# Inverse over k2: another PSUM bank, two copies, and sums between SBUF operands

## The chip, the cores and the metric

The kernel runs on one core of a Trainium2 chip. The metric is device time in microseconds (us) of one execution; the median of three runs before the change was 2562.01 us (2561.42 to 2562.07). The trace shown here comes from one profiled execution.

## What is computed

The input x has 8 batches of 3008 positions and 256 features. A spectral layer comes first: a real Fourier transform over the positions, a complex product with a 256 x 256 matrix plus bias, soft thresholding, and the inverse transform. Its output goes row by row through a gated feed-forward network (FFN).

```python
X = np.fft.rfft(x, axis=1)
Yr = Xr @ w_r - Xi @ w_i + b_r
Yi = Xr @ w_i + Xi @ w_r + b_i
Y = np.sign(Y) * np.maximum(np.abs(Y) - 0.01, 0.0)   # Yr and Yi apart
y = np.fft.irfft(Yr + 1j * Yi, n=3008, axis=1)
out = (silu(y @ w_gate) * (y @ w_val)) @ w_out       # 256 -> 1536 -> 256
```

## The kernel before, in words

The program has two stages. The transform (`transform`, until about 520 us) computes the spectral layer, with 3008 split as 47 x 64 so that each Fourier transform is a pair of small matrix products. The FFN (`gated_ffn`) follows and is not touched by the change.

The transform works in units that overlap like a pipeline. For each batch, 8 chunks of input are multiplied by a Fourier matrix over 47 (`first`, L516, PSUM banks ps_a and ps_z) and transposed by VectorE (`turn`, L521). For each of 96 pairs of k1 follow the transform over 64 (`second`, L558), the split of its result into a high and a low part (L606 to L611), three products with the weights (`sum`, L565, in PSUM bank ps_s; `mix`, L580), the addition of the bias (`spread`, L569, which reads ps_s), the copy to SBUF (`gather` and `rest`, L591), and the thresholding (`clip` L617, `shrink` L618).

The inverse over k2 (`backs`, L619 to L662) takes one pair or two pairs in turn, 64 times. `back` (L639) multiplies the real half into one PSUM bank and the imaginary half into a second; for the first 53 these are ps_x0 and ps_x1, for the last 11 ps_a and ps_z. Then `keep` (L643, ScalarE) copies the imaginary half to SBUF, and `plus` and `minus` (L648, VectorE) form sum and difference of the real half in PSUM and the copy. `store` (L653) sends the result z to DRAM.

The inverse over k1 (`unit`, 56 times in the transform) loads z back, multiplies (`tiles`, L711) into the same banks ps_x0 and ps_x1, and copies both out (`xt0`, `xt1`, L723, on ScalarE or VectorE, each 376 columns). So `back` has to wait for the copies of the `tiles` before it (`own`, L626), and `tiles` for the `minus` of the last `back` (`free`, L756). On TensorE the three stand in the fixed order `tiles`, `first`, `back` (`then`, `soon`).

All of this is written as named steps with needs, an estimated cost, one or more engines and a key. A list scheduler (`Plan.order`) gives each engine its order: a step starts when its needs are met, and of those that could start the one with the least key goes first. `SHIFT` (by kind), `LATER` (by kind and range) and `NUDGE` (by name) move keys, in slots of 5.5 us; `BIAS` moves the choice between engines. A step may take and free a named resource (`takes`, `frees`), and `wide` marks VectorE steps for which the planner reckons with GpSimd. Each engine runs its steps in the order found. In the head (`head`, L367) the loads of batch 0's chunks, of wa, wj and wr, and of bias and wf have keys too; the order found before is wa, wj, wr, then the eight chunks.

Of the kernel before, what the change touches and what calls it, by code (L numbers as in the profile page):

```python
# [9 lines left out]
F32 = mybir.dt.float32  # L10
# [3 lines left out]
ALU = mybir.AluOpType  # L14
# [31 lines left out]
SHIFT = {'add': -0.5, 'lower': -2.68, 'third': -0.5, 'turn5': -0.45, 'turn4': -0.36, 'turn0': 0.85, 'y_hi': -0.37, 'f': -1.7, 'out': 5.65, 'spread': -0.67, 'back': 2.36, 'raw': -0.72, 'second': -6.01, 'y_lo': 0.68, 'shrink': -1.75, 'z_in': 3.81, 'mix': 0.52, 'wr': -16.97, 'turn1': 0.1, 'tiles': 0.76, 'turn6': -0.16, 'wo': 9.39, 'x_sum': 4.59, 'sum': -2.3, 'flat_lo': -1.55, 'xt1': -4.21, 'x': 2.74, 'store': 0.3, 'turn': 1.34, 'wm': -32.33, 'bits down': -0.5, 'upper': 3.57, 'wj': -17.49, 'kept': -6.94, 'negate': -11.43, 'turn3': -2.97, 'unit': 10.52, 'wm_hi': -10.71, 'z': 0.5, 'bias': 6.32, 'wi_lo': -0.06, 'turn2': -1.38, 'x_hi': 2.79, 'clip': -0.54, 'xt0': 0.88, 'wa': -15.83, 'warm': 7.15, 'bits up': -1.5, 'f_lo': -0.43, 'wm_lo': 4.79, 'wi': -0.1, 'f_hi': 2.5, 'wf': -0.48, 'rest': 2.68, 'first': -1.1, 'bits': -0.71, 'flat_hi': 4.03, 'sums': -0.64, 'x_first': -4.78, 'early': 7.49, 'keep': 2.85, 'xf': -0.91, 'x_lo': 10.96, 'minus': -0.48, 'gather': 4.93, 'f_sum': -4.37, 'plus': 0.33}  # L46
# [3 lines left out]
    ('f_lo', 66, 80, 1.25),  # L50
    ('turn', 4, 16, 0.37),
    ('clip', 26, 38, 0.62),
    ('xt0', 26, 47, -0.76),
    ('second', 42, 72, -0.49),
    ('rest', 73, 76, 0.14),
    ('first', 8, 16, 0.25),
    ('turn3', 5, 10, -1.0),
    ('bits', 7, 14, -1.12),
    ('turn0', 8, 14, -1.0),
    ('x', 15, 19, -1.0),  # L60
    ('turn', 12, 14, -0.25),
    ('tiles', 67, 68, -0.5),
    ('out', 12, 15, 0.25),
    ('kept', 8, 11, -0.12),
    ('turn4', 11, 12, -0.5),
    ('turn3', 3, 5, 0.12),
    ('back', 7, 10, 0.12),
# [260 lines left out]
def transform(ctx, tc, front, ring, last, ps_, feed, xp, w_r, w_i, cb, wup_raw, wdn_raw, ca, cf, ci, cq, w21, wup_d, wdn_d, xt_d, d2):  # L328
# [201 lines left out]
    def pair(b, p):  # L530

        made = {}

        def tile(name, shape, dtype, tag, **kw):
            if name not in made:
                made[name] = sb.tile(shape, dtype, name=tag, tag=tag, **kw)
            return made[name]

        first = lambda x: x[:, :2].rearrange("p q c (k b) -> p (c k) q b", b=64)
        blocks = lambda x: x.rearrange("p (a b) -> p a b", b=64)  # L540
        flat = lambda x: x[:, 2].rearrange("p c a -> p (c a)")
        both = lambda: made["ps_b"].rearrange("p (a q b) -> p a q b", q=2, b=64)
        total = lambda: tile("f", [P, 2 * P], F32, "f", bufs=2)
        f_hi = lambda: tile("f_hi", [P, 3, 2, P], F32R, "f_hi", bufs=3)
        f_lo = lambda: tile("f_lo", [P, 3, 2, P], F32R, "f_lo", bufs=3)
        t = lambda: made_t.__setitem__(j, tile("t", [P, T], F32, "t", bufs=4)) or made_t[j]
        y = lambda: tile("y", [P, T], F32, "y", bufs=2)
        mixb = mixed[p % 2]

        def second(part=slice(0, 2)):  # L550
            if part.start == 0:
                made["ps_b"] = ps_.tile([P, T], F32, name="ps_b", tag="ps_b")
            ps = made["ps_b"]
            src = d1[b % 2][:, p]
            for cc in range(2)[part]:
                for k in range(2):
                    s = (cc * 2 + k) * P
                    nc.tensor.matmul(ps[:, s : s + P], lhsT=src[:, cc * P : (cc + 1) * P, k], rhs=wf[:, 2 * p + k, :], start=True, stop=True)  # L558

        def total_product():  # L560
            p1 = made["ps_s"] = ps_.tile([P, T], F32, name="ps_s")
            n = 0
            for cc in range(2):
                for w, x in PASSES:
                    nc.tensor.matmul(p1[:, :C], lhsT=(f_hi, f_lo)[x]()[:, 2, cc, :], rhs=wmix[0][w][:, cc, :], start=n == 0, stop=n == 5)  # L565
                    n += 1

        def spread():
            v.tensor_tensor(  # L569
                mixb.rearrange("p (a c) -> p a c", c=C),  # L570
                made["ps_s"][:, :C].rearrange("p (a c) -> p a c", a=1).to_broadcast([P, 2, C]),
                bias[0],
                op=ALU.add,
            )

        def mix():
            for half, (q, i) in enumerate(((1, 2), (0, 1))):
# [36 lines left out]
        add("mix", "PE", 1.45, 2.4, [now("spread"), now("f_lo")], mix)
        add("gather", "ACT", 0.74, 2.7, [now("mix"), back_of(j - 4) if j >= 4 else None], lambda: gather(0), tail=0.0)
        add("rest", "ACT", 0.74, 2.72, [now("gather")], lambda: gather(1), tail=0.0)
        add("clip", "DVE", 0.34, 2.95, [now("rest"), old("shrink", 2)], lambda: v.tensor_scalar(y(), t(), LAM, -LAM, op0=ALU.min, op1=ALU.max), wide=True)  # L617
        add("shrink", {"DVE": 0.61} if j > B * NP - 3 else {"POOL": 1.23, "DVE": 0.61}, None, 3.0, [now("clip")], lambda eng=v: eng.tensor_tensor(t(), t(), y(), op=ALU.subtract), wide=True)  # L618
    def backs(i):  # L619

        js = [3 * i // 2] if i % 2 == 0 else [3 * i // 2, 3 * i // 2 + 1]
        k = i + BEHIND
        n = len(js)
        box = {}
        key = 1.5 * k * SLOT
# [577 lines left out]
```

## Time and profile before

| what | value |
|---|---|
| median of 3 runs | 2562.01 us |
| profiled execution | 2560.62 us |
| span of its trace | 2558.5 us |
| mean granted TensorE clock | 0.999 |
| busy: TensorE / VectorE / GpSimd / ScalarE | 99% / 80% / 79% / 64% |

The span is the time from the first to the last instruction; the profiled execution is 2.1 us longer and 1.4 us shorter than the median. TensorE's matrix products overlap, and the ends that the profile gives are modelled, so its busy share hides short waits; the distance from one step's start to the next one's start shows them. PE is TensorE, PEld its weight loads, DVE VectorE, ACT ScalarE, POOL GpSimd, SP the engine that issues DMAs.

### The profile page before, as it was taken

To read this page: it belongs to the slowest core of one execution; us is meant where nothing else is said; L and a number is where in the kernel's file an instruction comes from. 1 tells how busy PE (TensorE), PEld (TensorE's weight loads), DVE (VectorE), ACT (ScalarE), POOL (GpSimd) and SP (SyncE) were. 2 spreads that over 40 slices of the span, in tenths; PEclk is the share of its full clock that TensorE was granted. 3 is DMA by queue.
4 is the path that set the end of the run, shared out by engine and by line. 5 is a ranking of instruction groups with operands and counts; after the bars stand their busy time and mean duration, and the time that the engine had idled before them with its cause. 6 is when DMAs were issued, how large, how long until landed. Compare 5 with 4: busy or idle time off the path is not lost.

```text
span 2558.5 us, 46813 instructions
## 1 busy us (share of the span) xinstructions
PE 2533.3 (99%) x16990; PEld 2101.3 (82%) x16990; DVE 2056.0 (80%) x3075; ACT 1626.3 (64%) x3188; POOL 2029.6 (79%) x1572
## 2 busy tenths in 40 slices
PE   8999999999999999999999999999999999999999
PEld 6777778878888888888888888888888888888899
DVE  6998888668777877887888788878787888788787
ACT  4676766756666666666666666665666566666665
POOL 4776665568888888888888888888888888888886
PEclk9999999999999999999999999999999999999999
DMA  6889887855445445544544444444444444444453
GB/s 212 270 272 284 288 283 249 269 204 192 164 156 170 158 158 160 168 154 148 167 163 150 142 163 163 150 142 163 163 149 142 158 163 146 142 160 159 150 183 123
DMA packets 134886, 460.55 MB, mean 180 GB/s; under 512 B 13824, under 2 KB 59904, under 8 KB 134656
## 3 DMA queue, kind: packets, MB, share of 16 engines
q1 hardware_dynamic: 134512, 457.46, 53.8%
q8 instruction: 135, 2.21, 0.3%
q14 instruction: 95, 0.78, 0.1%
q10 hardware_dynamic: 144, 0.10, 0.0%
HBM read 366.54 MB, written 90.96 MB: 179 GB/s over the span
## 4 chain that ended last, share of the span: by engine, by line
PE 79%; DVE 0%; ACT 0%; issue 0%; DVEq 0%; ACTq 0%
PE bank L860 79%; PE bank L1104 0%; PE ps_x L711 0%; DVE bank L1033 0%; DVE z L648 0%; PE ps_t L639 0%; DVE o L941 0%; DVE bank L1055 0%; DVE hidden L1055 0%; ACT part L643 0%; ACT xt L723 0%; DVEq L1193 0%; DVEq L1033 0%; ACTq L643 0%
## 5 line engine op out<-in xcount | busy, mean ns | idle before, releaser
L860 PE MATMUL bank<-x_near,wup 128*128 128x512 f32 (+1 forms) x4032 | 1035.7, 386 | 1.6 <-DVE z L648 1.0
L880 POOL TENSOR_TENSOR h_parts<-more,h_parts 128x512 fp32r<-128x512 f32 (+1 forms) x572 | 846.9, 1494 | 101.2 <-ACT h_parts L876 100.5
L860 PEld LDWEIGHTS bank<-x_near,wup 128*128 128x128 f32 x4032 | 750.9, 188 | 154.1 <-DVE bank L1033 4.1
L860 PE MATMUL bank<-h_parts,wdn 128*128 128x512 f32 (+1 forms) x3024 | 835.1, 385 | 0.0
L880 POOL TENSOR_TENSOR h_parts<-hidden,h_parts 128x512 fp32r<-128x512 f32 (+1 forms) x431 | 563.4, 1316 | 220.2 <-ACT h_parts L876 199.5
L860 PEld LDWEIGHTS bank<-h_parts,wdn 128*128 128x128 f32 x3024 | 564.8, 188 | 108.5 <-POOL h_parts L880 0.3
L876 ACT CAST h_parts<-hidden 128x512 fp32r<-128x512 f32 (+1 forms) x433 | 265.4, 613 | 451.7 <-DVE hidden L1006 451.7
L860 PE MATMUL bank<-x_parts,wup 128*128 128x512 f32 (+1 forms) x2016 | 525.5, 384 | 0.0
L1006 DVE TENSOR_TENSOR hidden<-hidden,bank 128x512 f32<-128x512 f32 (+1 forms) x576 | 376.1, 674 | 77.8 <-PE bank L860 69.5
L860 PEld LDWEIGHTS bank<-x_parts,wup 128*128 128x128 f32 x2016 | 375.4, 188 | 71.6 <-DVE bank L1033 1.7
L901 DVE TENSOR_TENSOR sums<-sums,bank 128x512 f32<-128x512 f32 (+1 forms) x357 | 240.3, 673 | 234.3 <-PE bank L860 234.3
L876 ACT CAST h_parts<-more 128x512 fp32r<-128x512 f32 (+1 forms) x572 | 349.3, 611 | 38.2 <-DVE more L871 27.0
L1004 ACT ACTIVATE hidden<-bank 128x512 f32<-128x512 f32 (+1 forms) x432 | 252.1, 584 | 115.4 <-PE bank L860 114.1
L871 DVE TENSOR_TENSOR more<-hidden 128x512 f32<-128x512 f32 (+1 forms) x286 | 291.2, 1057 | 0.0
L871 DVE TENSOR_TENSOR more<-hidden,more 128x512 f32<-128x512 f32 (+1 forms) x286 | 257.3, 900 | 0.0
L1011 ACT COPY bank<-bank 128x512 f32<-128x512 f32 (+1 forms) x288 | 161.6, 561 | 110.0 <-DVE hidden L1006 104.1
L1033 DVE TENSOR_TENSOR bank<-hidden,bank 128x512 f32<-128x512 f32 (+1 forms) x288 | 197.0, 684 | 39.4 <-PE bank L860 27.0
L618 POOL TENSOR_TENSOR t<-t,y 128x512 f32<-128x512 f32 x94 | 126.4, 1345 | 99.5 <-DVE y L617 87.9
L1019 ACT COPY hidden<-bank 128x512 f32<-128x512 f32 (+1 forms) x288 | 167.6, 582 | 2.4
L591 ACT COPY t<-mixb 64x256 f32<-64x256 f32 x384 | 140.7, 366 | 33.6 <-PE mixb L580 27.6
L284 POOL TENSOR_TENSOR x_near<-xf,x_near 128x512 fp32r<-128x512 f32 (+1 forms) x112 | 141.1, 1275 | 5.0 <-PE bank L860 4.8
L1055 DVE TENSOR_TENSOR hidden<-hidden,bank 128x512 f32<-128x512 f32 (+1 forms) x144 | 97.4, 676 | 43.9 <-PE bank L860 43.7
(94 smaller groups left out, 2868.3 us busy)
## 6 DMA issues: line engine op xcount, KB each, us to landing
wup<-wup_d SPq DMA_DIRECT2D x288, 896.0 KB, 4.6
scratch<-xp SPq DMA_DIRECT2D x59, 512.0 KB, 5.7
out<-o SPq DMA_DIRECT2D x88, 256.0 KB, 6.1
d<-z SPq DMA_DIRECT2D x84, 256.0 KB, 4.1
xt_d<-xt SPq DMA_DIRECT2D x56, 376.0 KB, 6.3
z_in<-d SPq DMA_DIRECT2D x98, 192.0 KB, 4.7
xf<-xt_d SPq DMA_DIRECT2D x15, 1024.0 KB, 6.8
wup_d<-wup SPq DMA_DIRECT2D x12, 896.0 KB, 5.0
```

The source lines that it names most:

```text
L284: low = lambda: eng.tensor_tensor(part[:, 1, :h], src, f32(part[:, 0, :h]), op=ALU.subtract)
L591: nc.scalar.copy(t()[64 * half : 64 * half + 64, k * C : (k + 1) * C], mixb[64 * k : 64 * k + 64, half * C : (half + 1) * C])
L860: nc.tensor.matmul(o, lhsT=weights[w], rhs=parts[x], start=start and i == 0, stop=stop and i == 2, skip_group_check=True)
L871: v.tensor_tensor(at(o, h), at(a, h), at(b, h), op=ALU.subtract)
L876: act.copy(pair[i][:, 0, :h], at(i, h))
L880: eng.tensor_tensor(pair[i][:, 1, :h], at(i, h), f32(pair[i][:, 0, :h]), op=ALU.subtract)
L901: v.tensor_tensor(o, o, spare[:, :h], op=ALU.add)
L1004: act.activation(at(i, h), src, AF.Silu)
L1006: v.tensor_tensor(at(i, h), at(i, h), src, op=ALU.mult)
L1011: act.copy(b3[:, :h], b1[:, :h])
L1019: act.copy(m5, b2[:, :h])
L1033: v.tensor_tensor(b2[:, :h], m5, b3[:, :h], op=ALU.add)
```

## The change

The imaginary half of the first 53 inverses over k2 goes to ps_s, the bank of `sum`, in place of ps_x1. `back` therefore needs `xt0` alone of the copies before it, and it shares the named resource "sums" with `sum`: `sum` takes it and `spread` frees it, `back` takes it and `keep` frees it. Both halves are now copied out of PSUM (`hold` for the real half, into z itself; `keep` for the imaginary half), each on ScalarE or VectorE. `minus` comes before `plus`, both read SBUF alone, and each may run on GpSimd or VectorE; `store` waits for `plus`. They are not marked `wide`. The next `back` waits for both copies, and the next `tiles` for `hold` and for the two xt copies before it.

All tables of keys are other ones. `NUDGE` has 24 entries (1620 before), `LATER` 21 (18 before), and `SHIFT` has other values for nearly every kind; the entries for the head's loads and weights ('wr', 'wj', 'wm', 'wm_hi', 'wa') go from between -10.7 and -32.3 slots to between -1.0 and 0.06, and 'x_first', 'early', 'wi', 'wf' and 'wm_lo' have none. With these keys the chunks of batch 0 stand ahead of wr and wj, and chunk 0 ahead of wa.

```diff
-        add("sum", "PE", 0.73, 1.3, [now("flat_lo"), old("spread", 1)], total_product)
-        add("spread", "DVE", 0.61, 1.45, [now("sum"), old("rest", 2)], spread)
+        add("sum", "PE", 0.73, 1.3, [now("flat_lo"), old("spread", 1)], total_product, takes="sums")
+        add("spread", "DVE", 0.61, 1.45, [now("sum"), old("rest", 2)], spread, frees="sums")
...
-        own = [f"xt0 {k - APART}", f"xt1 {k - APART}"] if APART <= k < PAIRS else []
+        own = [f"xt0 {k - APART}"] if APART <= k < PAIRS else []
...
-        before = [f"minus {i - 1}"] if i else []
+        before = [f"hold {i - 1}", f"keep {i - 1}"] if i else []
...
-            box["ps"] = [... for tag in (("ps_x0", "ps_x1") if k < PAIRS else ("ps_a", "ps_z"))]
+            box["ps"] = [... for tag in (("ps_x0", "ps_s") if k < PAIRS else ("ps_a", "ps_z"))]
...
-        def keep():
+        def copy(to, src, eng):
+            (nc.scalar.copy if eng is None else eng.tensor_copy)(to, src[:, : n * C])
+
+        def hold(eng):
+            box["z"] = sb.tile([P, 2, T], F32, name="z", tag="z", bufs=2)
+            copy(box["z"][:, 0, : n * C], box["ps"][0], eng)
+
+        def keep(eng):
             box["part"] = sb.tile([P, T], F32, name="part", tag="part", bufs=2)
-            nc.scalar.copy(box["part"][:, : n * C], box["ps"][1][:, : n * C])
-
-        def join(s, op):
-            if not s:
-                box["z"] = sb.tile([P, 2, T], F32, name="z", tag="z", bufs=2)
-            v.tensor_tensor(box["z"][:, s, : n * C], box["ps"][0][:, : n * C], box["part"][:, : n * C], op=op)
+            copy(box["part"][:, : n * C], box["ps"][1], eng)
+
+        def join(s, op, eng):
+            eng.tensor_tensor(box["z"][:, s, : n * C], box["z"][:, 0, : n * C], box["part"][:, : n * C], op=op)
...
-        plan.add(f"keep {i}", "ACT", 0.28 if n == 1 else 0.48, key + 0.4 * SLOT, ...)
-        plan.add(f"plus {i}", "DVE", 0.34 if n == 1 else 0.61, key + 0.5 * SLOT, [f"keep {i}"] + old, lambda: join(0, ALU.add))
-        plan.add(f"minus {i}", "DVE", 0.34 if n == 1 else 0.61, key + 0.55 * SLOT, [f"plus {i}"], lambda: join(1, ALU.subtract))
+        out_of = {"ACT": 0.28, "DVE": 0.34} if n == 1 else {"ACT": 0.48, "DVE": 0.61}
+        both = {"POOL": 0.7, "DVE": 0.34} if n == 1 else {"POOL": 1.23, "DVE": 0.61}
+        plan.add(f"hold {i}", out_of, None, key + 0.4 * SLOT, [f"back {i}"] + old, hold)
+        plan.add(f"keep {i}", out_of, None, key + 0.42 * SLOT, [f"back {i}"] + ([f"plus {i - 2}"] if i > 1 else []), keep, frees="sums" if k < PAIRS else None)
+        plan.add(f"minus {i}", both, None, key + 0.5 * SLOT, [f"keep {i}", f"hold {i}"], lambda eng: join(1, ALU.subtract, eng))
+        plan.add(f"plus {i}", both, None, key + 0.55 * SLOT, [f"minus {i}"], lambda eng: join(0, ALU.add, eng))
...
-        free = [f"minus {i - 1}"] if i > 0 and k <= PAIRS else []
+        free = ([f"hold {i - 1}"] if i > 0 and k <= PAIRS else []) + ([f"xt0 {k - 1 - APART}", f"xt1 {k - 1 - APART}"] if k > APART else [])
```

The biases of the new steps are 'hold DVE': 0.5, 'keep DVE': 1.1, 'minus DVE': -0.2, 'plus DVE': -1.5 (us added to the time at which VectorE would end, for the choice alone); that of 'xt0 DVE' is 3.8 and that of 'xt1 DVE' 1.1, where there were none. In `SHIFT`, 'hold' has 4.09 slots and 'keep' -0.58.

## Rows read from the trace of the kernel before

**Rows 1.** The page: span of the program, and the chain that ended last.

```profile
span 2558.5 us, 46813 instructions
...
PE bank L860 79%; PE bank L1104 0%; PE ps_x L711 0%; DVE bank L1033 0%; DVE z L648 0%; PE ps_t L639 0%; DVE o L941 0%; DVE bank L1055 0%; DVE hidden L1055 0%; ACT part L643 0%; ACT xt L723 0%; DVEq L1193 0%; DVEq L1033 0%; ACTq L643 0%
```

**Rows 2.** Windows: busy us of PE, PEld, DVE, ACT, POOL (instructions); clock; DMA share; GB/s.

```profile
0.00:24.00 24.00, 19.16 (x113) 8.05 (x114) 10.67 (x18) 4.77 (x8) 6.89 (x10) 0.86 0.79 289
...
95.00:450.00 355.00, 345.17 (x5441) 280.37 (x5441) 308.78 (x579) 244.96 (x596) 235.29 (x232) 1.00 0.87 278
```

**Rows 3.** Waits of PE's weight loads, 95 to 450 us: total, times, longest.

```profile
PEld ps_t L639 <- ACT xt L723: 22.2, 20, 1.3
PEld ps_t L639 <- DVE xt L723: 16.1, 22, 1.3
```

**Rows 4.** Timeline, three inverses: start, length, engine, line, operation [idle before].

```profile
311.51 1.07 PE L516 MATMUL ps_a<-scratch,wa 48*64 48x512 f32 x8
...
311.80 0.85 ACT L723 COPY xt<-ps_x 128x376 f32<-128x376 f32 x2
...
312.70 1.09 PE L639 MATMUL ps_t<-t,wi 64*64 64x256 f32 x16
...
339.75 1.07 PE L516 MATMUL ps_a<-scratch,wa 48*64 48x512 f32 x8
...
340.64 1.04 PE L639 MATMUL ps_t<-t,wi 64*64 64x256 f32 x16
...
349.19 1.07 PE L516 MATMUL ps_a<-scratch,wa 48*64 48x512 f32 x8
...
350.68 0.66 PE L639 MATMUL ps_t<-t,wi 64*64 64x256 f32 x8 [0.42 <-ACT xt L723]
```

**Rows 5.** Groups by line, 95 to 450 us: busy, mean | idle before.

```profile
L618 POOL TENSOR_TENSOR t<-t,y 128x512 f32<-128x512 f32 x68 | 92.5, 1361 | 67.0 <-DVE y L617 60.3 <-PE ps_a L516 6.7
...
L648 DVE TENSOR_TENSOR z<-ps_t,part 128x256 f32<-128x256 f32 (+1 forms) x90 | 47.8, 536 | 2.5 <-ACT part L643 2.1
...
L723 ACT COPY xt<-ps_x 128x376 f32<-128x376 f32 x66 | 29.2, 478 | 9.4 <-PE ps_x L711 7.8 <-ACT t L591 0.9
...
L643 ACT COPY part<-ps_t 128x512 f32<-128x512 f32 (+1 forms) x44 | 21.1, 479 | 22.3 <-PE ps_t L639 21.9
```

**Rows 6.** One line, 600 to 2500 us: VectorE operation with both operands in SBUF.

```profile
L871 DVE TENSOR_TENSOR more<-hidden x268: 544/949/1782, 604.2 to 2496.4; 128x512 f32<-128x512 f32 x127, 128x384 f32<-128x384 f32 x7
```

**Rows 7.** Timeline around the inverse at 312.70 us.

```profile
312.77 0.69 DVE L569 TENSOR_TENSOR mixb<-ps_s,bias 128x512 f32<-128x512 f32 x1
...
313.89 0.58 ACT L643 COPY part<-ps_t 128x512 f32<-128x512 f32 x1 [0.94 <-PE ps_t L639]
...
314.69 0.36 PE L565 MATMUL ps_s<-wm_hi,f_hi 128*128 128x256 f32 x1
```

**Rows 8.** Timeline of the head.

```profile
1.19 0.42 SPq L402 DMA_DIRECT2D wj<-w_i  x1
...
2.17 0.47 SPq L384 DMA_DIRECT2D scratch<-xp  x1
...
8.42 1.09 PE L516 MATMUL ps_a<-scratch,wa 48*64 48x512 f32 x8 [1.88 <-DMA scratch<-xp]
...
16.85 5.04 DVE L521 STREAM_TRANSPOSE d<-ps_a 128x512 f32<-128x512 f32 x8 [0.53 <-PE ps_a L516]
...
21.95 0.74 PE L558 MATMUL ps_b<-wf,d 128*128 128x128 f32 x4 [0.17 <-DVE d L521]
```

**Rows 9.** Timeline of the step from transform to FFN.

```profile
517.57 1.38 PE L711 MATMUL ps_x<-wo,z_in 48*64 48x47 f32 x64
...
517.92 0.58 ACT L643 COPY part<-ps_t 128x512 f32<-128x512 f32 x1 [0.17 <-PE ps_t L639]
518.54 1.29 DVE L648 TENSOR_TENSOR z<-ps_t,part 128x512 f32<-128x512 f32 x2 [2.00 <-ACT part L643]
...
519.97 1.63 PE L860 MATMUL bank<-x_near,wup 128*128 128x512 f32 x6 [1.03 <-DVE z L648]
```

More of the change, by code (lines that the diff above doesn't have):

```diff
@@ L45 @@
 FEED = 84
-SHIFT = {'add': -0.5, 'lower': -2.68, 'third': -0.5, 'turn5': -0.45, 'turn4': -0.36, 'turn0': 0.85, 'y_hi': -0.37, 'f': -1.7, 'out': 5.65, 'spread': -0.67, 'back': 2.36, 'raw': -0.72, 'second': -6.01, 'y_lo': 0.68, 'shrink': -1.75, 'z_in': 3.81, 'mix': 0.52, 'wr': -16.97, 'turn1': 0.1, 'tiles': 0.76, 'turn6': -0.16, 'wo': 9.39, 'x_sum': 4.59, 'sum': -2.3, 'flat_lo': -1.55, 'xt1': -4.21, 'x': 2.74, 'store': 0.3, 'turn': 1.34, 'wm': -32.33, 'bits down': -0.5, 'upper': 3.57, 'wj': -17.49, 'kept': -6.94, 'negate': -11.43, 'turn3': -2.97, 'unit': 10.52, 'wm_hi': -10.71, 'z': 0.5, 'bias': 6.32, 'wi_lo': -0.06, 'turn2': -1.38, 'x_hi': 2.79, 'clip': -0.54, 'xt0': 0.88, 'wa': -15.83, 'warm': 7.15, 'bits up': -1.5, 'f_lo': -0.43, 'wm_lo': 4.79, 'wi': -0.1, 'f_hi': 2.5, 'wf': -0.48, 'rest': 2.68, 'first': -1.1, 'bits': -0.71, 'flat_hi': 4.03, 'sums': -0.64, 'x_first': -4.78, 'early': 7.49, 'keep': 2.85, 'xf': -0.91, 'x_lo': 10.96, 'minus': -0.48, 'gather': 4.93, 'f_sum': -4.37, 'plus': 0.33}
+SHIFT = {'add': -0.5, 'lower': 3.45, 'third': -0.5, 'turn5': -2.56, 'turn4': -0.52, 'turn0': -0.23, 'y_hi': -0.37, 'f': 1.24, 'out': -2.32, 'spread': -1.87, 'back': 1.18, 'raw': -5.24, 'second': -4.82, 'y_lo': 0.68, 'shrink': -5.54, 'z_in': 0.06, 'mix': 0.55, 'wr': -1.0, 'turn1': 0.2, 'tiles': 0.94, 'turn6': -0.34, 'wo': 0.06, 'x_sum': 7.6, 'sum': -4.95, 'flat_lo': 1.38, 'xt1': 1.43, 'x': 3.03, 'store': -0.91, 'turn': 3.45, 'wm': -0.12, 'bits down': -0.5, 'upper': 2.97, 'wj': -0.12, 'kept': -7.82, 'negate': 0.25, 'turn3': 1.92, 'unit': -14.47, 'wm_hi': -0.12, 'z': 0.5, 'bias': -0.44, 'wi_lo': -0.06, 'turn2': 0.71, 'x_hi': 4.92, 'clip': 0.55, 'xt0': 0.98, 'wa': 0.06, 'warm': 0.25, 'bits up': -1.5, 'f_lo': 0.92, 'f_hi': 1.87, 'rest': 4.15, 'first': 4.34, 'bits': 1.7, 'flat_hi': 3.89, 'sums': 2.92, 'keep': -0.58, 'xf': 6.58, 'x_lo': -4.03, 'minus': 2.83, 'gather': 5.4, 'f_sum': -2.09, 'plus': 0.04, 'hold': 4.09}
 REACH = 160
@@ L49 @@
 LATER = [
[L50 to L66, printed above, removed]
@@ L70 @@
-BIAS = {'y_lo POOL': -2.0, 'z DVE': -16.1, 'flat_lo DVE': 12.3, 'shrink DVE': 3.4}
+    ('turn', 11, 18, 1.0),
+    ('sums', 6, 7, 0.99),
+    ('shrink', 21, 33, -2.25),
+    ('shrink', 22, 71, -0.62),
+    ('flat_lo', 65, 98, 1.5),
+    ('flat_hi', 54, 98, -0.87),
+    ('first', 5, 28, -2.37),
+    ('z_in', 29, 35, 1.25),
+    ('lower', 2, 6, -0.25),
+    ('bits', 1, 5, -0.5),
+    ('kept', 3, 12, 0.37),
+    ('plus', 12, 28, 0.87),
+    ('tiles', 58, 68, -0.12),
+    ('lower', 11, 12, 0.38),
@@ new lines @@
+    ('f_lo', 84, 96, 0.13),
+    ('second', 39, 57, -0.25),
+    ('kept', 7, 10, 0.5),
+    ('turn5', 6, 10, 0.25),
+    ('flat_lo', 86, 96, -0.5),
+    ('turn2', 10, 12, -1.0),
+    ('flat_lo', 14, 49, 0.12),
+]
+NUDGE = {'clip 25': 1.0, 'first 12': -1.0, 'second 6': 0.25, 'clip 37': -0.25, 'turn 5 4': 0.5, 'f_lo 89': 0.25, 'store 7': -0.25, 'sum 15': 1.0, 'hold 53': -0.5, 'tiles 50': 0.5, 'f_hi 9': 0.25, 'store 37': -0.25, 'f 56': -1.0, 'f 21': -0.5, 'gather 56': 0.25, 'x 7': 0.5, 'x 22': -1.0, 'minus 4': -0.25, 'store 3': -1.0, 'rest 46': 1.0, 'z_in 36': 0.25, 'out 22': -0.5, 'minus 56': -0.25, 'shrink 1': -0.25}
@@ L71 @@
+BIAS = {'flat_lo DVE': 1.4, 'shrink DVE': 1.7, 'xt0 DVE': 3.8, 'xt1 DVE': 1.1, 'hold DVE': 0.5, 'keep DVE': 1.1, 'minus DVE': -0.2, 'plus DVE': -1.5}
 SLOT = 5.5
@@ L625, in backs @@
         key = 1.5 * k * SLOT
-        own = [f"xt0 {k - APART}", f"xt1 {k - APART}"] if APART <= k < PAIRS else []
+        own = [f"xt0 {k - APART}"] if APART <= k < PAIRS else []
         turned = [f"turn {B - 1} {NCH - 1}"] if k >= PAIRS else []
-        before = [f"minus {i - 1}"] if i else []
+        before = [f"hold {i - 1}", f"keep {i - 1}"] if i else []
         def product():
-            box["ps"] = [ps_.tile([P, T], F32, name="ps_t", tag=tag) for tag in (("ps_x0", "ps_x1") if k < PAIRS else ("ps_a", "ps_z"))]
+            box["ps"] = [ps_.tile([P, T], F32, name="ps_t", tag=tag) for tag in (("ps_x0", "ps_s") if k < PAIRS else ("ps_a", "ps_z"))]
             for a, j in enumerate(js):
@@ L655, in backs @@
         old = [f"store {j - 3}" for j in js if j >= 3]
-        plan.add(f"back {i}", "PE", 0.483 * n, key + 0.15 * SLOT, [f"shrink {j}" for j in js] + own + turned + before, product, soon=[f"first {k + NCH // 2}" if k < PAIRS else f"tiles {k}"])
-        plan.add(f"keep {i}", "ACT", 0.28 if n == 1 else 0.48, key + 0.4 * SLOT, [f"back {i}"] + ([f"minus {i - 2}"] if i > 1 else []), keep)
-        plan.add(f"plus {i}", "DVE", 0.34 if n == 1 else 0.61, key + 0.5 * SLOT, [f"keep {i}"] + old, lambda: join(0, ALU.add))
-        plan.add(f"minus {i}", "DVE", 0.34 if n == 1 else 0.61, key + 0.55 * SLOT, [f"plus {i}"], lambda: join(1, ALU.subtract))
+        plan.add(f"back {i}", "PE", 0.483 * n, key + 0.15 * SLOT, [f"shrink {j}" for j in js] + own + turned + before, product, takes="sums" if k < PAIRS else None, soon=[f"first {k + NCH // 2}" if k < PAIRS else f"tiles {k}"])
+        out_of = {"ACT": 0.28, "DVE": 0.34} if n == 1 else {"ACT": 0.48, "DVE": 0.61}
[4 more added lines that the diff above has]
+        plan.add(f"plus {i}", both, None, key + 0.55 * SLOT, [f"minus {i}"], lambda eng: join(0, ALU.add, eng))
         for a, j in enumerate(js):
-            plan.add(f"store {j}", "SP", 0.45, key + (0.8 + 0.1 * a) * SLOT, [f"minus {i}"], lambda a=a, j=j: store(a, j), tail=3.0, moves=256 * MOVE)
+            plan.add(f"store {j}", "SP", 0.45, key + (0.8 + 0.1 * a) * SLOT, [f"plus {i}"], lambda a=a, j=j: store(a, j), tail=3.0, moves=256 * MOVE)
         return [f"shrink {j}" for j in js]
```

2 lines of the change are left out of this document (removed).

## The prediction

> **What bounds the kernel now.** I read the page first: the chain that ended last lies for 79% of the span of 2558.5 us on the FFN's products at L860 [rows 1]. The change doesn't touch them, so any gain or loss must come from the first 520 us. There I cut the time into stages with the windows view. From 95 to 450 us, where all parts of the transform run side by side, PE is busy for 345.2 of 355 us, DVE for 308.8, ACT for 245.0, POOL for 235.3, and the DMA engines 87% [rows 2]. TensorE is the bound, with VectorE not far behind, so a saved us counts only where TensorE waited for it, and a late VectorE step becomes such a wait soon.
>
> The waits view names the largest one. Weight loads of the inverse (L639) stood 22.2 us behind the xt copies on ScalarE and 16.1 us behind those on VectorE [rows 3]. This isn't all lost, since products of `first` still run in that time; what is lost shows in the timeline, in the distance from the start of `first` to the start of `back` [rows 4]. Undisturbed it is 0.89 us (339.75 to 340.64). Of the 44 inverses in the stretch 14 are like that. 17 are about 0.3 us later (311.51 to 312.70 is 1.19), 9 about 0.6 us later (349.19 to 350.68 is 1.49), 4 by 0.08 to 0.2 us. In the middle case the two xt copies run one after the other on ScalarE, from 311.80 to 312.65, and `back` starts 0.05 us after the second.
>
> **The change part by part.** *The bank.* Only `xt0` must be out now. One copy takes 0.478 us and both 0.85 [rows 4, 5], so the first ends 0.37 us before the second. The 17 lose their whole 0.30 (5.1 us), the 9 lose 0.37 each (3.3 us), the 4 some 0.14 each (0.6 us): 9.0 us. The bias of 3.8 us on 'xt0 DVE' keeps xt0 on ScalarE. If xt0 came second there, nothing would be gained; if the new order removed also the 0.23 that the 9 have left, it would be 11. So -9.0, between 0 and -11.
>
> *The price of the bank.* ps_s now belongs in turn to `sum` and to `back`. Ahead of `back` the last `spread` must have ended. In 13 of the 63 inverses that a sum precedes it had not: for the one at 312.70 it ended at 313.46 [rows 7]; these orders must change, and on VectorE the late step is moved past others. Behind `back`, the next `sum` must wait for `keep`. Now `keep` (313.89, 0.58 us) ends 0.22 us before that sum starts (314.69) [rows 7]; the middle one of all has 0.24 us, 11 end too late. Where `keep` goes to ScalarE at once, the sum isn't held; where another copy of the mean 0.48 us [rows 5] stands ahead of it, the sum is held for 0.48 - 0.22 = 0.26 us, or 14 us over 53. 'keep' has a much smaller shift than 'hold' (-0.58 against 4.09 slots), so it goes first; I take 0.045 us for each, +2.4 us, with 0 and +14 as ends. Below nothing it can't go: a wait is added, none taken away.
>
> *The copies and sums.* Before, ScalarE copied once (21.1 us in the stretch) and VectorE did two sums (47.8 us) [rows 5]. Now ScalarE gets most of a second copy, some 21 us, and by the biases most of VectorE's xt copies. It would be busy for about 276 of 355 us, so its queue stays open. The sums have the same mean 0.536 us on VectorE if nothing disturbs them; on GpSimd a full one takes up to 1.36 us by the nearest operation, L618 [rows 5]. No row of the transform has both operands of such a sum in SBUF on VectorE. The nearest is L871 in the FFN, with 0.544 us at least, 0.949 in the middle and 1.782 at most [rows 6]. VectorE's load in the stretch is 47.8 us lower if all goes to GpSimd and 47.8 x (0.949 / 0.675 - 1) = 19 us higher if all stays; 0.675 is a full sum of L648 in the same stretch, and the range stands for a VectorE busy for 261 to 328 us. Nobody on TensorE's path waits for `minus`, `plus` or `store` themselves; behind them on VectorE stand `spread`, `f_lo` and the transposes, for which TensorE does wait. I take +0.8 us, between -2 and +10.
>
> L871's spread over a factor of three shows what the sums may meet. The Trainium skill ("SBUF — State Buffer", Who interferes with whom) says why: a VectorE instruction with two SBUF inputs and a GpSimd instruction that reads SBUF exclude each other, and the second waits for the first to end. Before, one operand of the sums lay in PSUM, so by that rule they never waited. This speaks against the change; the rival "blocked" below is it.
>
> *The head.* wj and wr stood ahead of the first chunk; its DMA was issued at 2.17 us, and wj's at 1.19 [rows 8]. Issuing gives back 0.98 us. By bytes, 512 KB at the 289 GB/s of the first 24 us [rows 2] are 1.8 us. The first product waited 1.88 us for that chunk, and the head ends with transposes without a gap from 16.85 to 21.89, for which `second` waits at 21.95 [rows 8]; if all chunks come earlier, so does that end. wr and wj now land after the chunks, and five GpSimd steps of the weights hang on them; if these are late, the gain is gone and up to 1 us more. I take -1.2 us, from -1.8 to +1.
>
> *The step to the FFN.* The last TensorE step of the transform ends at 518.95, and the FFN starts at 519.97, after 1.03 us of waiting for `minus` [rows 9]. Now two copies free the banks: `keep` ended at 518.50, and `hold` can run beside it on VectorE, idle for 2.00 us. Of the wait -1.0 us goes; late is then the tiles product itself. If both copies go to ScalarE in turn, half remains.
>
> **Sum.** -9.0 + 2.4 + 0.8 - 1.2 - 1.0 = -8.0 us. From the profiled execution's 2560.6 us (2.1 us outside the span) that is 2552.6. The median of the runs was 1.4 us above that execution, so I predict 2554 us. All keys are new, and a new order moves small waits everywhere; that stands in the range, not in the sum.
>
> **Rivals.** *Blocked.* The sums on VectorE meet GpSimd, last 0.949 instead of 0.675 us, and hold up `spread` and `f_lo`. Two sums for 53 inverses are 0.55 us each and 29 us in all; a third of it reaching TensorE is 9.7 us, in place of the 0.8. That gives 2563 us: no change. For it: VectorE's 87% and L871's middle value; against it: GpSimd can take the sums, and 46 us of VectorE's stretch are idle [rows 2].
>
> *ps_s becomes the wait (slower).* The place is the sum after each `back`, and the `back` after a late `spread`. The gains are 11.2 us and the other cost 0.8, so slower by 5.1 us needs (11.2 - 0.8 + 5.1) / 53 = 0.29 us of wait per inverse. That is reached if `keep` regularly stands behind one other ScalarE copy (0.26) and a few of the 13 late spreads stay. With 0.4 us it is 21 us instead of 2.4, and 2573 us. For it: a margin of 0.22 us; against it: the planner knows both waits and reckons with them.
>
> *The change doesn't do what it says.* xt0 is copied late, behind the gathers that ScalarE has at that time, so that `back` starts when it did before. The 9.0 us fall away: 2563 us.
>
> *More.* The new order also closes waits that have nothing to do with xt: the 9.8 us without PE work in the stretch [rows 2] and as much hidden behind overlapping products. Half of 20 us more gives 2544 us.
>
> **How the numbers follow.** The forecast as reckoned has 0.47 (its own range 2548 to 2559), more 0.15, blocked 0.13, no effect of the bank 0.09, ps_s slower 0.16. To hold 8 in 10 the range goes from 2543, which leaves out half of "more", to 2567, which leaves out nearly all of "slower". A measurement of this kernel can tell 0.2%, 5.1 us: faster is below 2556.9, slower above 2567.1. Faster is four fifths of the forecast's case (0.39), all of "more" (0.15) and a little of "blocked" (0.06): 0.60. Slower is 0.16, and the same the rest, 0.24.
>
> **What would show it.** In the profile after, L639's wait for xt should fall from 38 us to below 15, and the distance from `first` to `back` be 0.89 us nearly everywhere. Waits of L565 for the copies on ScalarE or VectorE, and of L639 for L569, are the price; over 5 us of them the sum is wrong, over 15 the slower rival holds. VectorE's sums near 0.95 us show blocking. The FFN's first product should follow the last tiles without a gap, and the first `first` start near 7.2 us instead of 8.42. The prediction is wrong if PE's stretch between 95 and 450 us isn't shorter by some 6 us.

## The result: slower by 28 us, and the profile after

The changed kernel takes 2590.13 us (median of four runs, 2586.88 to 2592.78), the kernel before, measured beside it, 2561.82: 1.011 times as long, with an interval of 1.0093 to 1.0128. The prediction said 2554 us, with a range to 2567. It was wrong in sign and in size.

The page of the changed kernel: its span, and the chain that ended last.

```profile
span 2591.0 us, 46868 instructions
...
PE bank L871 78%; PE bank L1115 0%; DMA xt_d<-xt 0%; DVE bank L1044 0%; ACT xt L734 0%; DVE o L952 0%; DVE bank L1066 0%; DVE hidden L1066 0%; ACT bank L1022 0%; DVEq L1204 0%; DVEq L1044 0%; ACTq L734 0%; ACT part L645 0%
```

The FFN's products (now L871) still end the chain, as in [rows 1]. They start at 551.13 us instead of 519.97 [rows 9] and last as long as before to within 1.4 us (2591.0 - 551.1 against 2558.5 - 520.0). So the loss lies in the transform (31.2 us between these two executions; the medians differ by 28.3). Lines are shifted: `back` is L642, the sums L656, both copies L645, `spread` L572, `mix` L583, `clip` L620, `tiles` L722, f_lo on GpSimd L614, `shrink` L621, the xt copies L734.

The windows view of the changed kernel, with the columns of [rows 2]:

```profile
0.00:24.00 24.00, 19.28 (x135) 8.68 (x136) 13.34 (x22) 6.15 (x12) 7.32 (x11) 1.00 0.85 307
95.00:450.00 355.00, 331.93 (x5086) 267.64 (x5084) 319.55 (x527) 252.92 (x622) 248.61 (x227) 0.98 0.82 262
```

In the head more is done than before (135 matmuls against 113). In the middle stretch, where TensorE was busy for 345.2 us, it is busy for 331.9 and does 5086 matmuls in place of 5441, 6.5% fewer in the same time. VectorE is busier by 10.8 us and GpSimd by 13.3 us, though both finish fewer units. Followed by the start of `mix`, pair by pair, the changed kernel is 2.2 us ahead at pair 16 (102.0 against 104.2 us), 6.7 behind at pair 24, 13.1 at pair 32, 23.6 at pair 56 and 26.5 at pair 72. Most of it builds up in the stretch where all parts run side by side, though not evenly. Another 7.6 us come at one spot behind it: the loss is 24.5 us when `mix` of pair 83 starts (481.95 us) and 32.1 at pair 84. There ScalarE waits 3.55 us for the DMA that loads the FFN's first input, and TensorE 3.2 us for f_lo behind it.

Groups of the changed kernel by line and shape, 95 to 450 us: count | busy us, mean ns | idle before.

```profile
L620 DVE TENSOR_SCALAR y<-t 128x512 f32<-128x512 f32 x64 | 38.4, 601 | 3.2 <-ACT t L594 2.6 <-POOL scratch L479 0.4
L656 DVE TENSOR_TENSOR z<-z,part 128x512 f32<-128x512 f32 x39 | 35.1, 900 | 0.8 <-ACT z L645 0.5
L656 DVE TENSOR_TENSOR z<-z,part 128x256 f32<-128x256 f32 x40 | 34.0, 851 | 2.2 <-ACT z L645 2.0
...
L614 POOL TENSOR_TENSOR f_lo<-f,f_hi 128x256 fp32r<-128x256 f32 x63 | 56.2, 892 | 41.0 <-ACT f_hi L613 41.0
```

The answering groups of the kernel before, in the same view and stretch:

```profile
L617 DVE TENSOR_SCALAR y<-t 128x512 f32<-128x512 f32 x67 | 32.1, 479 | 3.4 <-ACT t L591 3.2
L648 DVE TENSOR_TENSOR z<-ps_t,part 128x512 f32<-128x512 f32 x44 | 29.6, 675 | 2.4 <-ACT part L643 2.1
L648 DVE TENSOR_TENSOR z<-ps_t,part 128x256 f32<-128x256 f32 x46 | 18.2, 403 | 0.2
...
L611 POOL TENSOR_TENSOR f_lo<-f,f_hi 128x256 fp32r<-128x256 f32 x67 | 49.9, 744 | 37.8 <-ACT f_hi L610 34.0 <-DVE y L617 3.0
```

The half-width sums have doubled (403 to 851 ns), the full ones grown by a third (675 to 900), and 79 of them cost 69.1 us where 90 cost 47.8 ([rows 5] gave them in one group). GpSimd's f_lo, which nobody edited, grew from 744 to 892 ns. Split by whether a GpSimd instruction ran at the same time, the full-width sums after take 967 ns beside one (30 of them) and 675 alone (9), the half-width ones 862 beside one (39) and 419 alone (a single one). Before, the half-width ones took 402 beside one (37) and 408 alone (9). So it is the meeting that costs these sums, and only where both operands lie in SBUF. The Trainium skill ("SBUF — State Buffer", Who interferes with whom) states that a VectorE instruction with two SBUF inputs contends with a GpSimd instruction that reads SBUF; the trace agrees.

The waits view, 95 to 450 us: total us, times, longest. First the changed kernel, then the one line of the kernel before.

```profile
PE mixb L583 <- DVE mixb L572: 10.5, 8, 2.6
...
PEld ps_t L642 <- ACT xt L734: 31.1, 36, 1.5
PEld mixb L583 <- DVE mixb L572: 11.0, 16, 2.1
```

```profile
PE mixb L580 <- DVE mixb L569: 2.0, 6, 0.4
```

TensorE's `mix` waits 10.5 us for `spread` on VectorE (2.0 us before), and the weight loads of `back` still stand 31.1 us behind xt, all of it on ScalarE, against 22.2 and 16.1 in [rows 3]. How a longer step becomes such a wait is seen in one place. The timeline of the changed kernel, VectorE first, then GpSimd, then TensorE:

```profile
160.61 0.99 DVE L656 TENSOR_TENSOR z<-z,part 128x512 f32<-128x512 f32 x1
161.52 0.70 DVE L524 STREAM_TRANSPOSE d<-ps_a 128x512 f32<-128x512 f32 x1
162.16 0.64 DVE L656 TENSOR_TENSOR z<-z,part 128x512 f32<-128x512 f32 x1
162.72 2.31 DVE L620 TENSOR_SCALAR y<-t 128x512 f32<-128x512 f32 x1
...
165.28 0.69 DVE L572 TENSOR_TENSOR mixb<-ps_s,bias 128x512 f32<-128x512 f32 x1
...
159.76 1.29 POOL L621 TENSOR_TENSOR t<-t,y 128x512 f32<-128x512 f32 x1
161.01 1.18 POOL L614 TENSOR_TENSOR f_lo<-f,f_hi 128x256 fp32r<-128x256 f32 x1
162.15 2.60 POOL L492 TENSOR_TENSOR wup<-scratch,wup 128x896 fp32r<-128x896 f32 x1
...
166.12 0.55 PE L583 MATMUL mixb<-wm_hi,f_hi 128*128 128x256 f32 x1 [2.62 <-DVE mixb L572]
166.47 0.41 PE L583 MATMUL mixb<-wm_hi,f_lo 128*128 128x256 f32 x1
```

The sum at 160.61 starts 0.44 us before GpSimd's L621 ends and lasts 0.99 us in place of 0.68; f_lo, which starts 0.4 us into the sum, ends 0.59 us after it. Then `clip`, 0.42 us when alone, starts beside GpSimd's L492 and ends 0.28 us after that ends, 2.31 us long. Behind it in VectorE's queue stands `spread`, which TensorE has waited for since the end of its last product: 2.62 us. And this wait has a second price. Windows of the changed kernel:

```profile
162.30:165.70 3.40, 1.20 (x11) 1.00 (x9) 3.40 (x4) 2.27 (x7) 3.04 (x2) 1.00 0.30 105
165.70:169.10 3.40, 2.98 (x14) 3.01 (x15) 3.30 (x5) 0.15 (x2) 2.65 (x3) 0.50 0.86 327
```

After 3.4 us with 1.20 us of work TensorE is granted 0.50, the 1.2 GHz level, for the next 3.4 us, and its products there start 0.21 us apart instead of 0.12. This happens four times between 95 and 450 us (ahead of the other three TensorE was busy for 1.6 to 2.0 us of 3.4) and for 6.8 us at 486.6; the kernel before had it only in its head.

### The profile page after: what moved, and what is told of

The parts are those of the page before. It is cut to its first block, busy times and chain, and to the rows that moved or that the text cites. A ratio compares the mean times of both kernels' runs of the same rounds, so it can differ in the third digit from the quotient of the medians.

```text
span 2591.0 us, 46868 instructions
## 1 busy us (share of the span) xinstructions
PE 2547.2 (98%) x16992; PEld 2109.4 (81%) x16992; DVE 2092.2 (81%) x3052; ACT 1656.3 (64%) x3271; POOL 2059.0 (79%) x1576
## 4 chain that ended last, share of the span: by engine, by line
PE 78%; DMA 0%; DVE 0%; ACT 0%; issue 0%; DVEq 0%; ACTq 0%
PE bank L871 78%; PE bank L1115 0%; DMA xt_d<-xt 0%; DVE bank L1044 0%; ACT xt L734 0%; DVE o L952 0%; DVE bank L1066 0%; DVE hidden L1066 0%; ACT bank L1022 0%; DVEq L1204 0%; DVEq L1044 0%; ACTq L734 0%; ACT part L645 0%
## 5 line engine op out<-in xcount | busy, mean ns | idle before, releaser
L871 PE MATMUL bank<-x_near,wup 128*128 128x512 f32 (+1 forms) x4032 | 1036.0, 386 | 1.8 <-ACT bank L1022 1.3
L871 PEld LDWEIGHTS bank<-x_near,wup 128*128 128x128 f32 x4032 | 750.8, 188 | 154.3 <-DVE bank L1044 4.0
L871 PE MATMUL bank<-h_parts,wdn 128*128 128x512 f32 (+1 forms) x3024 | 835.3, 385 | 0.0
L871 PEld LDWEIGHTS bank<-h_parts,wdn 128*128 128x128 f32 x3024 | 565.0, 188 | 108.3 <-POOL h_parts L891 0.3
L871 PE MATMUL bank<-x_parts,wup 128*128 128x512 f32 (+1 forms) x2016 | 525.7, 384 | 0.0
L1017 DVE TENSOR_TENSOR hidden<-hidden,bank 128x512 f32<-128x512 f32 (+1 forms) x576 | 376.1, 674 | 77.9 <-PE bank L871 69.5
L871 PEld LDWEIGHTS bank<-x_parts,wup 128*128 128x128 f32 x2016 | 375.3, 188 | 71.7 <-DVE bank L1044 1.6
L621 POOL TENSOR_TENSOR t<-t,y 128x512 f32<-128x512 f32 x94 | 128.8, 1371 | 88.7 <-DVE y L620 84.3
L614 POOL TENSOR_TENSOR f_lo<-f,f_hi 128x256 fp32r<-128x256 f32 x96 | 85.9, 895 | 73.6 <-ACT f_hi L613 73.6
```

What stands on the lines that cost most here:

```text
L871: nc.tensor.matmul(o, lhsT=weights[w], rhs=parts[x], start=start and i == 0, stop=stop and i == 2, skip_group_check=True)
L1017: v.tensor_tensor(at(i, h), at(i, h), src, op=ALU.mult)
```

## The experiments

Theories: **blocked**, the sums with both operands in SBUF and GpSimd hold each other up, and this costs most of the 28 us; **bank**, the shared ps_s makes `sum` and `back` wait; **order**, the new keys and biases are worse, whatever is computed. "Order after" below means that all engines keep the instruction order of the changed kernel, "order before" that of the kernel before.

**1 to 3, in the order after.**

```
a1_psum_operand:  real = box["ps"][0] if eng is v else box["z"][:, 0]     # VectorE's sums: one operand in PSUM
a2_bank_x1:       ("ps_x0", "ps_s") -> ("ps_x0", "ps_x1")
a3_psum_x1:       both
```

> The changed kernel in its own order of steps on every engine, but VectorE's sums read the real half in PSUM as before the change (the copy into z is still made; the few sums on GpSimd still read SBUF). Theory 'blocked' (sums with both operands in SBUF and GpSimd's operations wait for each other; VectorE's sums took 69 us instead of 42 in the stretch 95 to 450 us): sums fall back to 0.40 and 0.68 us, GpSimd's f_lo from 0.89 to 0.75, and the time to 2565 or below. Rival 'order' (the new tables give a worse order whatever the operands): 2583 to 2590. Rival 'bank' (waits through ps_s): 2583 to 2590.

> The changed kernel in its own order of steps, but the imaginary half goes to ps_x1 again, so that the inverse waits for both xt copies and no longer shares ps_s. 'Blocked': 2590 to 2600, as the wait for the second copy (0.37 us for some 40 inverses, up to 15 us) comes back and nothing goes. 'Order': the same. 'Bank': below 2580.

> The changed kernel's order of steps with both undone: sums read PSUM, imaginary half in ps_x1. What is left of the change is the order (the new tables) and the second copy on ScalarE. 'Blocked': 2565 to 2575. 'Order': 2585 to 2600. 'Bank': below 2580.

Measured: a1 2584.80 us (1.0084, 1.0069 to 1.0099), a2 2592.73 (1.0116, 1.0101 to 1.0131), a3 2595.05 (1.0124, 1.0109 to 1.0139). a2 and a3 refute *bank*: with ps_x1 back nothing is regained (a2 can't be told from the changed kernel, a3 is 10.3 us slower than a1). a1 and a3 are misses for *blocked*, and lie where *order* expected them: in a1 the sums are back at 678 and 411 ns and f_lo at 756, but only some 5 us come back. Its waits view, 95 to 450 us, shows where the rest went (`tiles` is L723 here, the sums L657):

```profile
PE ps_x L723 <- DVE z L657: 13.0, 14, 2.3
```

In this order `tiles` may start once the bank has been copied out; with sums that read the bank it must wait for them, and their places in VectorE's queue are late. TensorE idles as long ahead of `tiles` in a3 (13.5 us, of which the profile puts none down to the sums). The edit put one wait in the place of another, so the question had to be asked without it, in the order before.

**4 to 6, in the order before.**

```
b2_sbuf_sums:  keep() also copies ps[0] to z[:, 0]; join reads z[:, 0] and part (minus first, then plus)
b3_copies:     the same second copy; join reads ps[0] and part, as before
b1_bank:       ("ps_x0", "ps_x1") -> ("ps_x0", "ps_s"), nothing else
```

> The kernel before in its own order of steps and banks, with the copies and the sums between SBUF operands alone: ScalarE copies both halves in the place of the one, VectorE forms minus and plus from SBUF in the place of the two sums. 'Blocked': 2575 to 2590, with VectorE's sums near 0.85 to 0.90 us in the middle. 'Order': 2562 to 2568 (only a second copy on ScalarE more). 'Bank': 2562 to 2568.

> The kernel before in its own order, with the second copy on ScalarE as in the run b2_sbuf_sums, but minus and plus read the real half in PSUM. It differs from that run only in where one operand of the sums lies. 'Blocked': 2561 to 2567, with VectorE's sums at 0.40 and 0.68 us. Rival 'second copy' (ScalarE's queue gets 21 us more in the stretch and passes it on to TensorE): 2580 to 2588, as in b2_sbuf_sums.

> The kernel before in its own order, with the imaginary half in ps_s and nothing else. The inverse no longer waits for the second xt copy (9.0 us by the prediction's sum), but 13 spreads end late (0.8 us each, 10 us) and 11 sums start before the copy ends (0.6 us each, 7 us), since this order was not made for it. 'Bank' (ps_s itself is what costs): 2575 or above. 'Blocked' and 'order' both: 2558 to 2570.

Measured: b2 2588.51 us (1.0096, 1.0079 to 1.0113), b3 2565.96 (1.0015, 1.0006 to 1.0025), b1 2564.83 (1.0014, 1.0005 to 1.0023). b2 and b3 have the same copies and the same order and differ only in where the sums read the real half, and b2 is 22.6 us slower (21.3 us, if each is taken against the kernel before measured beside it). Their sums in the groups by line, 95 to 450 us, first b2, then b3:

```profile
L648 DVE TENSOR_TENSOR z<-z,part 128x512 f32<-128x512 f32 x40 | 37.0, 924 | 7.7 <-ACT z L645 7.5
L648 DVE TENSOR_TENSOR z<-z,part 128x256 f32<-128x256 f32 x42 | 33.4, 796 | 1.1 <-ACT z L645 0.8
```

```profile
L648 DVE TENSOR_TENSOR z<-ps_t,part 128x512 f32<-128x512 f32 x44 | 29.9, 682 | 9.2 <-ACT z L645 9.2
L648 DVE TENSOR_TENSOR z<-ps_t,part 128x256 f32<-128x256 f32 x44 | 17.7, 412 | 1.2 <-ACT z L645 0.9
```

The second copy alone (b3) costs about 4.5 us, the bank alone (b1) about 3.4, in an order made for neither. In this order the operands' place is nearly the whole loss.

**7. One operand in the order after.** The sums on VectorE become 32x32 transposes with one SBUF operand, in the same places and with the same bank; the kernel no longer forms the sums.

```
if eng is v: v.transpose(box["z"][:, s, : n * C], (box["z"][:, 0] if s else box["part"])[:, : n * C])
```

> The changed kernel in its own order, with VectorE's sums replaced by transposes of 32 x 32 blocks that read one SBUF operand (minus reads z, plus reads the copied imaginary half): the output is wrong, the needs, the bytes written and the order stay, the bank is freed by the copy as in the changed kernel. 'Blocked': the replaced operations take 0.4 and 0.7 us in place of 0.85 and 0.90, and the time falls by 15 us or more, to 2575 or below. 'Order': 2584 to 2590.

Measured: 2571.10 us (1.0036, 1.0022 to 1.0049). Groups by line, the window and a line of the waits, 95 to 450 us:

```profile
L657 DVE STREAM_TRANSPOSE z<-part 128x512 f32<-128x512 f32 x22 | 15.3, 697 | 0.0
...
L657 DVE STREAM_TRANSPOSE z<-part 128x256 f32<-128x256 f32 x22 | 9.4, 427 | 0.0
...
L614 POOL TENSOR_TENSOR f_lo<-f,f_hi 128x256 fp32r<-128x256 f32 x67 | 50.9, 760 | 38.1 <-ACT f_hi L613 37.9
```

```profile
95.00:450.00 355.00, 342.76 (x5419) 277.61 (x5418) 307.88 (x550) 268.31 (x658) 240.97 (x234) 1.00 0.86 282
```

```profile
PE mixb L583 <- DVE mixb L572: 1.0, 3, 0.6
```

As many steps in the same queue, nearly as long as the old sums, but with one operand: 19.0 of the 28.3 us are gone, f_lo is back at 760 ns, the clock at 1.00, and TensorE at 342.8 us. The wait of `mix` for `spread` falls from 10.5 us to 1.0. 9.6 us are left. The trace shows where most of them arise: `mix` of pair 83 starts 4.6 us later than in the kernel before and that of pair 84 11.1 later, at the spot where the changed kernel lost 7.6. Timeline of a4_one_input:

```profile
465.05 0.62 ACT L286 CAST x_near<-xf 128x512 fp32r<-128x512 f32 x1 [3.35 <-DMA xf<-xt_d]
...
467.74 0.39 PE L568 MATMUL ps_s<-wm_hi,f_lo 128*128 128x256 f32 x1 [3.01 <-POOL f_lo L614]
```

The kernel before has no such wait of ScalarE. No run takes it away, so what it is worth isn't shown.

**8. The head.** The order before with only the head's keys of the change (wr, wj and the steps on them behind the chunks).

```
SHIFT: 'wr', 'wj', 'wm', 'wm_hi', 'negate', 'wa', 'bias', 'warm' from the changed kernel; 'x_first', 'early', 'wi', 'wf', 'wm_lo' left out
```

> The kernel before with the head's keys of the changed one alone (chunks ahead of wr and wj). In the changed kernel's trace the head ended 3.7 us earlier (its second weight product of the first pair at 18.28 us in place of 21.95) at a granted clock of 1.00 in place of 0.86. If that is worth as much without the rest: 2557 to 2559. If the order behind it loses as much: 2561 to 2564.

Measured: 2563.30 us (1.0009, 1.0000 to 1.0018), so no gain. But the keys alone don't bring the changed kernel's head: the `second` that started at 18.28 us there and at 21.95 before starts at 21.36, and `mix` of pair 0 1.8 us later than before, where the changed kernel has it 1.4 us earlier. By pair 16 the difference is under 1 us.

**9 to 11. Where else the sums can go, and the rest.**

```
a7_minus_pool:  BIAS 'minus DVE': -0.2 -> 2.0
a8_both_pool:   BIAS 'minus DVE' and 'plus DVE': 3.0
a9_one_x1:      a4_one_input with ("ps_x0", "ps_x1")
```

> The changed kernel with one bias altered ('minus DVE' from -0.2 to 2.0), so that about half of the sums go to GpSimd. In the changed kernel GpSimd took three sums in the stretch 95 to 450 us, of 1.18 us (256 columns) and 1.73 us (512), against 0.85 and 0.90 us on VectorE. 'Blocked': half the sums leave VectorE, which gets some 35 us less, but GpSimd gets 40 x 1.45 = 58 us more (249 to some 307 of 355 us) of the kind that reads two operands in SBUF, and each meets VectorE's other steps with two operands in SBUF; the loss is not undone, 2580 to 2600 us. 'Order' (the loss is in the new keys and biases, and the sums on VectorE only lengthen beside other work): with VectorE relieved by 35 us the time falls towards 2571, what the kernel without two-operand sums took.

> The changed kernel with both biases of the sums at 3.0, so that nearly all sums go to GpSimd. 80 sums of 1.18 to 1.73 us are 116 us more on GpSimd in the stretch 95 to 450 us, which then has 365 us of work in 355: GpSimd becomes the bound, and its `shrink` and `f_lo` come late. 'Blocked': slower than the changed kernel, over 2600 us. 'Order': VectorE, relieved by some 69 us, sets TensorE free, and the time is 2570 to 2585.

> The kernel in which VectorE's sums are replaced by 32x32 transposes with one operand (its output is not the sums), and in addition the imaginary half of the inverse goes to ps_x1, its bank before the change. It asks where the 9.6 us come from that the transposes left over the kernel before (2571.1 against 2561.5). 'Bank' (the shared ps_s makes sums wait for copies): the 9.6 us fall, 2562 to 2566. 'Order' (the bank costs nothing, and the rest is the order and the second copy): no gain, 2569 to 2578, since `back` must wait for both xt copies again.

Measured: a7 2592.32 us (1.0114, 1.0099 to 1.0129), a8 2597.96 (1.0138, 1.0123 to 1.0153), a9 2577.48 (1.0061, 1.0045 to 1.0078). a7, with half of the sums of the stretch on each engine, stays where the changed kernel was. a8 has all 82 sums of the stretch on GpSimd, which is busy for 326 of 355 us, while VectorE falls to 283. It was expected over 2600 and came 2 us below. The relief of VectorE gains nothing. What stays there meets GpSimd instead; but GpSimd, now 92% busy, is late as well (it idles 1.6 us ahead of f_lo, where it idled 41.0), and which of the two keeps TensorE isn't told apart. a8, groups by line:

```profile
L620 DVE TENSOR_SCALAR y<-t 128x512 f32<-128x512 f32 x63 | 47.2, 749 | 7.9 <-ACT t L594 7.2
```

`clip` has one operand in SBUF and lengthens all the same: in the changed kernel it takes 732 ns beside a GpSimd instruction (38 of 64) and 409 without (26). The Trainium skill ("SBUF — State Buffer", Who interferes with whom) lists `tensor_scalar` among the operations that can enter a mode in which VectorE uses the port pair it shares with GpSimd, and so can contend; the trace agrees.

a9 lies 6.4 us above a4: in this order the shared bank is worth something, and the 9.6 us don't come from it.

**12 to 14. An order that knows of it.** The planner reckons with such a meeting for `clip` and `shrink` (`wide=True`), not for the sums.

```
a10_told:      both sums wide=True; BIAS 'minus DVE': -0.2 -> -1.5
a12_untold:    BIAS 'minus DVE': -0.2 -> -1.5
a11_told_dve:  both sums wide=True; BIAS 'minus DVE' and 'plus DVE': -3.0
```

> The changed kernel with both sums marked in the planner as `clip` and `shrink` are (a step that waits for GpSimd's step before it, and holds up its next), and the bias of `minus` at -1.5 like that of `plus`, so that all sums stay on VectorE. 'Order that does not know': the sums are put into GpSimd's pauses or reckoned with, `spread` and `f_lo` no longer come late by surprise; half of the 19 us comes back, 2575 to 2582. 'Operands alone': GpSimd is busy for 249 of 355 us, so few pauses are there to be used; the sums still last 0.85 to 0.95 us on the mean, TensorE waits as before, 2586 to 2600.

> The control for the kernel with marked sums: the bias of `minus` at -1.5, no marks. By both theories near the changed kernel, 2585 to 2596, since only the three sums of the stretch that went to GpSimd move to VectorE; how far it is from 2590 says how much a new order alone moves the time.

> As the kernel with marked sums, with the two biases at -3.0: a second order with the same marks. 'Order that does not know': 2575 to 2582 again. 'Operands alone': 2586 to 2600. If it lies more than 6 us from the first, the order's chance is as large as the effect, and the two together decide nothing finer than that.

Measured: a10 2610.09 us (1.0187, 1.0170 to 1.0204), a12 2594.35 (1.0128, 1.0113 to 1.0143), a11 2610.75 (1.0190, 1.0174 to 1.0206). Both theories missed: told of the meeting, the order is worse by 16 us than its control. It does what was asked: the sums shrink to 833 and 754 ns in a10 (885 and 855 in a12). But `spread` comes no earlier and f_hi later. The waits view of a10:

```profile
PE mixb L583 <- DVE mixb L572: 12.5, 15, 2.8
PE mixb L583 <- ACT f_hi L613: 5.5, 3, 2.4
```

In the control these are 11.3 and 1.5 us.
The keys and nudges had been fitted without the mark, so this doesn't show what the best order with it could do. It shows that the mark alone regains nothing.

## Why the prediction was wrong, step by step

**The bound** was read rightly: TensorE in the first 520 us, with VectorE close behind, so that a late VectorE step soon becomes TensorE's wait.

**The failed step is the price of the sums.** It stood in the sum as +0.8 us, between -2 and +10, and measured 22.6 us in the order before (b2 against b3) and 19.0 in the order after (the changed kernel against a4). The mechanism was named, as the rival *blocked*, and its sign of life, sums near 0.95 us, came. Of the 21.8 us between 0.8 and 22.6, 8.9 were given away when the rival's own 9.7 us, which already made the case no gain, were set aside. The argument for that, that GpSimd could take the sums, failed: the planner left it three of 82 in the stretch, and a8, with all of them there, is no faster.

The other 12.9 us the rival's working missed. Its 29 us on VectorE, for the two sums of 53 inverses, were nearly right: these take 32.7 us longer in b2 than in b3. (The factor of 1.4 that L871's full-width steps gave was laid on all sums; the full ones grew by 1.33, the half-width ones by 2.11.) But the last 11 inverses got such sums too, which makes 38.8 us between b2 and b3 (107.9 against 69.1 in 128 sums) and 36.0 between the changed kernel and the one before (104.3 in 124 against 68.3 in 128), and f_lo on GpSimd, longer by 148 ns in each of 63, wasn't counted. And the third of it that was to reach TensorE was a guess: 22.6 of 38.8 us are 58%, and 19.0 of 36.0 are 53%. What came by VectorE's longer steps and what by GpSimd's no run tells apart. The price makes 18 to 22 of the 36 us by which the forecast was off; the rest lies in the bank, whose gain didn't come, and in the order.

**The bank, -9.0 and +2.4.** Against the kernel before, the gain didn't come. The start of `back` after `first` should have been 0.89 us nearly everywhere; of 39 inverses in the stretch 13 are there, 14 are 0.23 us late, 8 by 0.3 to 0.5 and 4 by more, 10.0 us in all, as much as before (11.1, by the counts in the prediction). Only xt0 is needed now, but all xt copies are on ScalarE and start later in this order, so `back` waits for the first copy where it waited for the second. At 187.07 us the two begin, 0.77 us after `first` (0.29 at 311.51 in [rows 4]), and `back` follows the end of the first by 0.05 us. This is the rival *doesn't do what it says*, in part. In one and the same order the bank is worth something: 6.4 us (a9 against a4), 10.3 (a3 against a1) and 2.6 (a2 against the changed kernel, within the noise), net of its price; the prediction's net was 6.6. The price, weight loads of `back` behind a late `spread`, is 5.4 us in 6 waits with 3.0 us of idle TensorE; `sum` nowhere waits long for a copy. So *ps_s becomes the wait* is refuted (a2), though its sign was the right one. The prediction's counts for this price, 13 late spreads and 11 late copies, took in the last 11 inverses, which never use ps_s; of the first 53 it is 8 and 6. *More* found nothing: TensorE's time without work in the stretch grew from 9.8 to 23.1 us.

**The head, -1.2.** At its place it gave more: the first product starts at 6.11 us instead of 8.42, and `second`, at 21.95 in [rows 8], at 18.28; `mix` is ahead by 1.4 us at pair 0 and by 3.6 at pair 8. By pair 24 the loss has swallowed the lead. What it would be worth without the loss isn't shown, for e6 lost it before the first `mix`.

**The step to the FFN, -1.0,** is right in size. The timeline of the changed kernel:

```profile
549.69 1.51 PE L722 MATMUL ps_x<-wo,z_in 48*64 48x47 f32 x64
550.08 0.58 ACT L645 COPY z<-ps_t 128x512 f32<-128x512 f32 x1
550.56 0.59 ACT L645 COPY part<-ps_t 128x512 f32<-128x512 f32 x1
551.13 1.66 PE L871 MATMUL bank<-x_near,wup 128*128 128x512 f32 x6
```

Both copies went to ScalarE in turn, and still the first product follows `tiles` without the 1.03 us of [rows 9]: it starts 0.02 us before the second copy ends, so it doesn't wait for that one. The half that the prediction left in this case isn't there.

**The order** stood in the range alone. 9.6 us are left without two-operand sums (a4). Up to pair 80 a4 is 3.5 us behind the kernel before, and 6.5 us come between pairs 83 and 84, at ScalarE's wait for the FFN's input. The second copy costs about 4.5 us by b3, if it costs the same in this order, and `clip` meets GpSimd more often than before (585 ns on the mean in a4 against 479). How the 9.6 us divide among these isn't settled, since no run takes one of them alone away. In the chances, four fifths of 0.47 are 0.38, not 0.39, which changes nothing here.

None of these kernels beats the one before.

## What to carry over

Before an operand is moved from PSUM to SBUF to free a bank, look at what GpSimd does at that time: the second copy alone was cheap here (4.5 us), but a VectorE sum that had one operand in PSUM may double, and lengthens GpSimd's steps as well. VectorE was 87% busy and stands ahead of TensorE in every unit, and of the load added to it more than half arrived there (53% and 58%), so a mechanism that adds some 30 us decides the sign and belongs in the sum. And a wait that vanishes in the code is gained only if the order then lets the remaining one come earlier.

## Hardware that was not expected

The meeting stretches both sides on the mean: VectorE's sums from 403 to 851 ns and GpSimd's f_lo from 744 to 892. It also catches `clip`, with one operand and no PSUM: 409 ns alone, 732 beside GpSimd, 2.31 us where it started beside a GpSimd step of 2.60. TensorE's granted clock halved for 3.4 us after single stretches of low work, such as 1.20 us in 3.40, so a wait of 2.62 us on VectorE costs more than its length: the 12 products of that `mix` start some 0.09 us further apart, about 1 us in all by estimate.
